# Whole-array sums and masks, and an output projection in two banks, in a recurrent attention kernel

## The chip, the cores and the metric

The kernel runs on one core of a Trainium2 chip. A core has five engines that work side by side and wait for each other through semaphores: TensorE (in the profile PE for matmuls and PEld for the weight loads that go ahead of them), VectorE (DVE), ScalarE (ACT), GpSimd (POOL) and SyncE (SP), which only starts transfers here. Matmuls write to PSUM, which has eight banks of 128 partitions x 512 fp32 numbers; DVE and ACT copy results from there to SBUF. The metric is the device time of one execution in microseconds (us). Three executions of the kernel before took 796.89, 798.72 and 798.89 us, so the median is 798.72 us.

## What is computed

The input x has 2048 rows of 512 numbers. The output is g * a + (1 - g) * b, where g is a sigmoid gate for each row, b is a layer norm followed by a two-layer MLP (512 to 1376 to 512), and a is an attention with a memory, which goes through x in 64 segments of 32 rows:

```
mem = mem0                                   # 8 rows of 512
for s in range(64):
    h = concat(mem, x[32*s : 32*s+32])       # 40 rows
    q, k, v = h @ Wq, h @ Wk, h @ Wv         # 32 heads of 128
    p = softmax(where(mask, q k^T / sqrt(128), -1e9))    # 40 x 40 a head
    o = (p v) @ Wo                           # 4096 -> 512
    mem, out[s] = o[:8], o[8:]
```

The memory rows of one segment are an input of the next one, so the 64 steps form a chain. All matrix inputs are bf16.

## The kernel before

There are two stages. The MLP for all 2048 rows runs first (about 110 us) and leaves (1 - g) * b in DRAM. Then comes the loop over the 64 segments, which is nearly all of the rest. T = s // 4 is the tile of 128 rows that a segment lies in, si = s % 4 its place in the tile.

**Column tiles.** A step's rows are few: 32 (the 8 memory rows and 24 of the segment; the other 8 rows of each of four segments, called left, are projected together once per tile). So most matmuls use only 32 of the array's 128 columns, and four of them are placed side by side with `tile_position=(0, 32 * j)`: each loads 128 x 32 weights into its own quarter of the columns and writes its own 32 PSUM partitions. Four such matmuls are called a quad here. The profile shows a column tile as `128*32`, a matmul over the whole array as `128*128`, and a matmul with 32 contracted rows (a row tile) as `32*128`.

**One step of the loop, in the order of TensorE.** The order of every engine's queue is the order of the program (`manual_schedule`), and each engine works its own queue in order.
- Q and K of the step (`qk_unit`, L110): 16 quads of 512 columns into banks U0 to U3. Between the first four quads and the rest stands `mask_mm(1)` (L248): it writes the additive mask of heads 16 to 31 into bank W, as four column tiles of 224 columns, with a quarter of the identity as weights in each.
- `scores(s, 0)` (L256, L260) adds q k^T onto the mask that lies in bank SbF; ACT takes the exponentials.
- V of the step (`v_unit`, L129), eight quads of 512 columns in banks X1 and X2. After five of these eight, `msum(0)` calls `sums` (L267, L270): two quads with the block-diagonal matrix of ones BO as weights, each of 32 columns, which sum the exponentials over the keys of each of the four heads. DVE takes the reciprocal (L668) and scales E in place (L669). After one more quad of V comes `scores(s, 1)` on bank W, then the last two quads of V, then `msum(1)`.
- `run(W1)`: two quads of side work, `fill`, on banks X1 and X2: projections of the left rows of the next tile (L110, L129), or the output projection of the left rows of the previous tile (L141). A step has eight quads of it, given out two at a time.
- The sums of the other queries (`sums(xsum, ...)`): two quads, of 256 and 64 columns, into SbF.
- `av` (L280, L285): p v in row tiles, in two halves. The second half waits for the scaled E of `mnorm(1)`.
- ACT copies the memory part of U0 to U3 to UT (L697) and then the rest to XR (L598). TensorE does two more quads of side work.
- `wo_pass` (L619): the output projection, eight groups of one quad each (`wo_group`, L141), 512 columns, all into bank W. ACT copies W to w (L622).
- `mask_mm(0)` for the next step, into SbF; two quads of side work; in some steps `extra`: four whole-array transposes of x at si = 3 (L156), or the assembly of a finished output tile at si = 0 (L226 and L228).
- Four whole-array matmuls of 8 columns (L709) with w as weights add up the four partial sums and transpose the memory rows. DVE copies them to hT (L710), which the Q of the next step waits for. The last two quads of side work stand between.

The last step, after the loop, has its own code (L718 to L755): on DVE a reciprocal (L723), two products that scale E (L726, L727), and on TensorE one `wo_pass` for the step before it, ahead of `av`, and another one for itself near the end.

Of the kernel before, what the change touches and what calls it, by code (L numbers as in the profile page):

```python
# [27 lines left out]
def kernel(ctx, tc, A_x, A_mem0, A_Wq, A_Wk, A_Wv, A_Wo, A_seg_len, B_x, B_w1, B_b1, B_w2, B_b2, gate_w, out):  # L28
    nc = tc.nc
    P = 128  # L30
    _, S, Dm = A_x.shape
# [29 lines left out]
    Wo_sb = pers.tile([P, H, Dm], BF16)  # L61
    ident = pers.tile([P, P], BF16)
# [12 lines left out]
    Mk = ep.tile([P, 4, EW], BF16)  # L75
    BO = ep.tile([P, P], BF16)
# [16 lines left out]
    U = [lps.tile([P, 512], FP32, name=f"U{i}") for i in range(4)]  # L93
# [3 lines left out]
    W = lps.tile([P, 512], FP32)  # L97

    Sb = [bk[:, 0:4 * EW].rearrange("p (i c) -> p i c", c=EW) for bk in (SbF, W)]
# [34 lines left out]

    HORD = [(j, ih) for j in (0, 2, 1, 3) for ih in range(2)]

    def wo_group(bk, U_, n):
        j, ih = HORD[n]
        for c in range(4):
            i = 4 * ih + c  # L140
            nc.tensor.matmul(bk[32 * c:32 * c + 32, :], lhsT=U_[:, j, i, :], rhs=Wo_sb[:, 4 * i + j, :],  # L141
                             start=(n == 0), stop=(n == NW - 1), tile_position=(0, 32 * c))

    NW = len(HORD)
# [66 lines left out]
    def wo_left(T, bk):  # L211
        for n in range(NW):
            wo_group(bk, UL[T % 2], n)
            if n < NW - 1:
                yield

        def ca():
            wl = cw.tile([P, Dm], BF16, tag="wl", name="wl")
            nc.scalar.copy(out=wl[:], in_=bk[:])
            wls[T] = wl  # L220
        act_q.append(ca)
        yield
# [21 lines left out]
                              in_=QL[T % 2][:].bitcast(FP32).rearrange("p a (l s) b -> p a l s b", s=SPT)[:, :, :, si])  # L244

    def mask_mm(i2):
        for j in range(4):
            nc.tensor.matmul(Sb[i2][32 * j:32 * j + 32], lhsT=ident[:, 32 * j:32 * j + 32], rhs=Mk[:],  # L248
                             start=True, stop=True, skip_group_check=True, tile_position=(0, 32 * j))

    def scores(s, i2):
        T, si = divmod(s, SPT)
# [10 lines left out]
                             start=False, stop=True, skip_group_check=True, tile_position=(0, 32 * j))  # L263

    def sums(out, E, c_main, c_left, n, start):
        for j in range(4):
            nc.tensor.matmul(out[32 * j:32 * j + 32], lhsT=BO[:, 32 * j:32 * j + 32], rhs=E[:, :, c_main:c_main + n],  # L267
                             start=start, stop=False, skip_group_check=True, tile_position=(0, 32 * j))
        for j in range(4):
            nc.tensor.matmul(out[32 * j:32 * j + 32, :, n - 8:n], lhsT=BO[:, 32 * j:32 * j + 32], rhs=E[:, :, c_left:c_left + 8],  # L270
                             start=False, stop=True, skip_group_check=True, tile_position=(0, 32 * j))

    def av(s, V, E):
        T, si = divmod(s, SPT)
# [286 lines left out]
    nc.gpsimd.memset(rmin[:], 1.0)  # L561

    mask_mm(0)
    Rs = {}
    fill = iter(())
# [50 lines left out]
                                in0=XR[:, :, RIDE:32], in1=Rb[:, :, RIDE:32], op=ALU.mult)  # L616

    def wo_pass(U_):
        for n in range(NW):  # L619
            wo_group(W, U_, n)  # L620
        w = cw.tile([P, Dm], BF16, tag="w", bufs=8, name="w")
        nc.scalar.copy(out=w[:], in_=W[:])  # L622
        return w

    W1, W2, W3 = 2, 2, 2
    for s in range(nseg):
# [17 lines left out]
        for n, (t, hf) in enumerate(((0, 0), (1, 0), (0, 1), (1, 1))):  # L644
            bk = U[n]
            for kc in range(KC):
                qk_unit(bk, hc, t, hf, kc)
            if n == 0:
                flush(act_q, 9)
                mask_mm(1)  # L650
                flush(dve_q, 9)
            qk_tr(qk_cast(bk[:]), (QT, KT)[t], hf)
        V = cw.tile([P, NG, Dh], BF16, tag="V", name="V")
        E = cw.tile([P, NG, EW], BF16, tag="E", name="E")
# [8 lines left out]
        def msum(i2):  # L663
            sums(U[i2][:, 320:352].rearrange("p (i q) -> p i q", q=8), E[:, 4 * i2:4 * i2 + 4, :], 8, 0, 8, True)
# [26 lines left out]
        mnorm(1)  # L691
        run(W1)
        sums(xsum, E, 16, 48, 32, True)
        recip_x(s)
        av(s, V, E)
# [3 lines left out]
        run(W2)  # L699
        prep_q(s + 1)  # L700
        w = wo_pass(UT[s % 2])
        if s >= 1:
            ws[s - 1] = w
        mask_mm(0)
        run(W3)
        for _ in extra(T, si):
# [10 lines left out]

    nx = slice(8 * NG, 40 * NG)  # L718
    sums(xsum, E, 16, 48, 32, True)
    for _ in out_sel(T - 1, X2):  # L720
        pass
    nc.gpsimd.memset(UL[T % 2][:, :, :, LEFT * si:seg], 0.0)
    nc.vector.reciprocal(out=R[:, nx], in_=SbF[:, 0:32 * NG])  # L723
    ws[s - 1] = wo_pass(UT[s % 2])
    Rr = R[:, nx].rearrange("p (i q) -> p i q", q=32)
    nc.vector.tensor_tensor(out=E[:, :, 16:48], in0=E[:, :, 16:48], in1=Rr, op=ALU.mult)  # L726
# [16 lines left out]
    nc.vector.tensor_scalar(out=good[:, 0:1], in0=tot[:, 0:1], scalar1=R_MIN, scalar2=None, op0=ALU.is_gt)  # L743
    nc.vector.tensor_scalar(out=good[:, 1:2], in0=tot[:, 1:2], scalar1=RSUM_MAX, scalar2=None, op0=ALU.is_lt)
    wf = wo_pass(UF)
    nc.tensor.matmul(X1[0:1, 0:1], lhsT=good[:, 0:1], rhs=good[:, 1:2], start=True, stop=True)
    bad = okp.tile([1, 1], I32)
    nc.vector.tensor_scalar(out=bad[:], in0=X1[0:1, 0:1], scalar1=-1.0, scalar2=float(P), op0=ALU.mult, op1=ALU.add)
    nc.tensor.matmul(X2[:], lhsT=SelL[:], rhs=wls.pop(T)[:], start=True, stop=False, skip_group_check=True)
    for i in range(SPT):  # L750
        nc.tensor.matmul(X2[32 * i:32 * i + 32, :], lhsT=(SelR if i < si else SelI)[:], rhs=(ws.pop(SPT * T + i) if i < si else wf)[:],
                         start=False, stop=True, skip_group_check=True, tile_position=(0, 32 * i))
# [126 lines left out]
```

## Time and profile before

One execution was profiled. Its own time was 799.05 us, with 797.3 us from its first to its last instruction.

| | us or count |
|---|---|
| median of the three times | 798.72 |
| profiled execution, own time and span | 799.05 and 797.3 |
| PE busy | 771.9 (97%), 18417 matmuls |
| PEld busy | 421.3 (53%), 18446 loads |
| ACT busy | 578.5 (73%) |
| DVE busy | 444.3 (56%) |
| POOL busy | 260.6 (33%) |
| granted TensorE clock, mean | 0.996 |
| one step of the loop, from one `scores(s, 0)` to the next | 10.89 |

The step's length is the distance of two rows of the trace: the first matmul of `scores` starts at 403.93 us in one step and at 414.82 us in the next.

The lines of the profile are read so. A group of instructions gives its source line, engine and operation, then out<-in by the program's names, the shapes, the count, and the mean time of one; for a matmul that time runs to its modelled end, which is long after the next one can start. A row of the timeline gives a start and a duration in us, the engine, the source line and how many instructions are merged in it; for the pace of TensorE the starts are to be compared, not the durations. A bracket tells how long the engine was idle ahead of the row and what it waited for.

### The profile page before, as it was taken

The numbers are of one execution on the slowest core, as the hardware profiler recorded it, in microseconds if no ns is written. First come the engines' busy times: TensorE is split into PE (matmuls) and PEld (weight loads), VectorE is DVE, ScalarE is ACT, GpSimd is POOL, SyncE is SP. The second block draws the span as 40 slices with busy tenths as digits, with TensorE's granted clock in tenths as the row PEclk, the third lists the DMA queues.
The fourth block names the chain that finished last, engine by engine and source line by source line (L and its number), as shares of the span: only waits on it lengthen the run. The fifth ranks groups of instructions, "written<-read, shape, count | busy, mean of one in ns | idle before, by whom it ended". The sixth has DMA issues, their size and how long they took to land.

```text
span 797.3 us, 41370 instructions
## 1 busy us (share of the span) xinstructions
PE 771.9 (97%) x18417; PEld 421.3 (53%) x18446; DVE 444.3 (56%) x1061; ACT 578.5 (73%) x1440; POOL 260.6 (33%) x391
## 2 busy tenths in 40 slices
PE   7999999999999999999999999999999999999996
PEld 5666554555555555555555555555555555555543
DVE  5776355555555554556555555655465556555554
ACT  4666677777777777777777777777777777777763
POOL 3111133333333334233333334333323333333331
PEclk9999999999999999999999999999999999999999
DMA  5779311212111222211121211222221212121111
GB/s 188 266 275 362 124 51 60 73 60 86 60 64 57 76 70 76 69 56 60 60 86 60 86 59 57 65 76 70 72 74 54 63 59 86 60 80 60 60 53 58
DMA packets 38151, 70.42 MB, mean 88 GB/s; under 512 B 3979, under 2 KB 27888, under 8 KB 36432
## 3 DMA queue, kind: packets, MB, share of 16 engines
q1 hardware_dynamic: 36448, 64.97, 24.6%
q8 instruction: 146, 2.39, 1.3%
q0 software_dynamic: 720, 1.97, 0.7%
q10 hardware_dynamic: 800, 0.79, 0.3%
q14 instruction: 37, 0.30, 0.1%
HBM read 59.06 MB, written 4.45 MB: 80 GB/s over the span
## 4 chain that ended last, share of the span: by engine, by line
PE 93%; ACT 3%; DVE 1%; issue 1%; DMA 1%; POOL 0%; SPq 0%; DVEq 0%; POOLq 0%; ACTq 0%
PE U L110 28%; PE X L129 18%; PE W L141 14%; PE X L110 7%; PE U L468 5%; PE U L280 4%; PE X L141 3%; ACT w L622 3%; PE W L462 3%; PE SbF L462 3%; PE W L709 2%; PE W L256 1%; PE U L267 1%; PE SbF L256 1%; PE SbF L267 1%
## 5 line engine op out<-in xcount | busy, mean ns | idle before, releaser
L115 ACT CAST Tb<-U 128x512 bf16<-128x512 f32 x258 | 195.2, 757 | 43.3 <-PE U L110 24.7
L614 POOL TENSOR_TENSOR UT<-XR,Rb 128x768 bf16<-128x768 bf16 x63 | 104.8, 1664 | 239.1 <-DMA Rb<-r_dr 199.4
L110 PEld LDWEIGHTS <-hT 128*32 128x32 bf16 x4096 | 103.7, 97 | 109.9 <-DVE hT L710 19.2
L129 PE MATMUL X<-Wv_sb,hT 128*32 128x512 bf16 x2048 | 136.4, 378 | 0.0
L110 PE MATMUL U<-Wq_sb,hT 128*32 128x512 bf16 x2048 | 132.7, 379 | 1.1 <-DVE hT L710 1.1
L110 PE MATMUL U<-Wk_sb,hT 128*32 128x512 bf16 x2048 | 132.7, 379 | 0.0
L141 PE MATMUL W<-Wo_sb,UT 128*32 128x512 bf16 x2080 | 124.6, 380 | 1.5 <-ACT UT L697 1.2
L608 POOL TENSOR_TENSOR racc<-racc,R 128x320 f32<-128x320 f32 x63 | 54.5, 866 | 181.9 <-DVE R L603 177.4
L603 DVE RECIPROCAL R<-SbF 128x256 f32<-128x256 f32 x63 | 110.3, 1751 | 0.0
L119 DVE STREAM_TRANSPOSE QT<-Tb 128x256 f32<-128x256 f32 x128 | 57.0, 445 | 80.8 <-ACT Tb L115 80.1
L119 DVE STREAM_TRANSPOSE KT<-Tb 128x256 f32<-128x256 f32 x128 | 57.0, 446 | 54.8 <-ACT Tb L115 54.8
L141 PEld LDWEIGHTS <-UT 128*32 128x32 bf16 x2080 | 57.1, 96 | 57.7 <-issue 19.7
L710 DVE CAST hT<-W 128x32 bf16<-128x32 f32 x63 | 12.1, 192 | 133.3 <-PE W L709 114.8
L598 ACT CAST XR<-U 128x256 bf16<-128x256 f32 x252 | 78.6, 438 | 0.0
L622 ACT CAST w<-W 128x512 bf16<-128x512 f32 x65 | 38.1, 585 | 45.3 <-PE W L141 45.3
L697 ACT CAST UT<-U 128x64 bf16<-128x64 f32 x252 | 35.3, 227 | 43.6 <-PE U L285 43.6
L129 PEld LDWEIGHTS <-hT 128*32 128x32 bf16 x2048 | 46.0, 95 | 20.5 <-issue 0.2
L115 ACT CAST Tb<-X 128x512 bf16<-128x512 f32 x62 | 46.3, 747 | 13.5 <-PE X L110 13.4
L668 DVE RECIPROCAL R<-U 128x32 f32<-128x32 f32 x126 | 45.0, 357 | 16.2 <-PE U L270 9.6
L267 PEld LDWEIGHTS <-BO 128*32 128x32 bf16 x760 | 32.2, 94 | 34.7 <-issue 13.4
L468 PE MATMUL U<-w_sb,hTm 128*128 128x512 bf16 (+1 forms) x163 | 49.5, 381 | 0.6
L462 PEld LDWEIGHTS <-w_sb 128*128 128x128 bf16 (+1 forms) x352 | 34.7, 102 | 21.0 <-issue 4.1
(152 smaller groups left out, 1207.7 us busy)
## 6 DMA issues: line engine op xcount, KB each, us to landing
Rb<-r_dr SPq DMA_DIRECT2D x63, 512.0 KB
Wv_sb<-in_A_Wv_dram SPq DMA_DIRECT2D x4, 1024.0 KB
Wq_sb<-in_A_Wq_dram SPq DMA_DIRECT2D x4, 1024.0 KB
Wk_sb<-in_A_Wk_dram SPq DMA_DIRECT2D x4, 1024.0 KB
Wo_sb<-in_A_Wo_dram SPq DMA_DIRECT2D x4, 1024.0 KB
VP<-VL SPq DMA_DIRECT2D x64, 64.0 KB
xt<-in_A_x_dram SPq DMA_DIRECT2D x16, 128.0 KB
xs<-in_A_x_dram SPq DMA_DIRECT2D x16, 128.0 KB
```

The costliest lines, as they stand in the source:

```text
L110: nc.tensor.matmul(bk[32 * j:32 * j + 32, :], lhsT=G[:, kc, :], rhs=W5[t][:, kc, h0:h1, j, :], start=(kc == 0), stop=(kc == KC - 1), tile_ ...
L115: nc.scalar.copy(out=Tb[:].rearrange("p a e b -> p a b e"), in_=bk.rearrange("p (a b e) -> p a b e", a=8, b=2))
L119: nc.vector.transpose(out=dst[:, 8 * hf:8 * hf + 8, 0:32, :].rearrange("p a r b -> p a (r b)").bitcast(FP32), in_=Tb[:].rearrange("p a e b ...
L129: nc.tensor.matmul(bk[32 * j:32 * j + 32, :], lhsT=G[:, kc, :], rhs=Wv5[:, kc, 4 * vb:4 * vb + 4, j, :], start=(kc == 0), stop=(kc == KC - ...
L141: nc.tensor.matmul(bk[32 * c:32 * c + 32, :], lhsT=U_[:, j, i, :], rhs=Wo_sb[:, 4 * i + j, :], start=(n == 0), stop=(n == NW - 1), tile_po ...
L462: nc.tensor.matmul(hp[:rows, 0:TB * P], lhsT=w1_sb[:, kc, fc * P:fc * P + rows], rhs=yTs[blk][:, kc, :], start=(kc == 0), stop=(kc == KC - 1))
L468: nc.tensor.matmul(bp(blk, tt)[:], lhsT=hTm[blk % 2][:rows, fc, tt * P:(tt + 1) * P], rhs=w2_sb[:rows, fc, :], start=(fc == 0), stop=(fc = ...
L598: nc.scalar.copy(out=XR[:, j], in_=U[j][:, 0:NG * 40].rearrange("p (i q) -> p i q", q=40)[:, :, 8:40])
L603: nc.vector.reciprocal(out=R[:, 8 * NG:], in_=SbF[:, 0:32 * NG])
L608: nc.gpsimd.tensor_tensor(out=racc[:], in0=racc[:], in1=R[:], op=ALU.add)
L614: nc.gpsimd.tensor_tensor(out=UT[(s + 1) % 2][:].rearrange("p j i q -> p (j i) q")[:, :, M:32], in0=XR[:, :, 0:RIDE], in1=Rb[:, :, 0:RIDE] ...
L622: nc.scalar.copy(out=w[:], in_=W[:])
```

## The change

Three functions change.
- `mask_mm` writes the mask with one matmul over the whole array (the 128 x 128 identity as weights) in place of four column tiles. The columns are 224 as before.
- `sums` uses the whole matrix BO as weights: two whole-array matmuls in place of two quads. BO is block-diagonal, so the result is the same.
- `wo_pass` makes the output projection in two passes over the eight groups. The first computes columns 0 to 383 in bank W, the second columns 384 to 511 in bank U0. ACT copies the 384 columns to w once the first pass is done, DVE the 128 columns after the second. The number of matmuls and weight loads of the projection doubles; the columns that they stream stay the same in sum.

```diff
-    def wo_group(bk, U_, n):
+    def wo_group(bk, U_, n, d=slice(0, 512)):
         j, ih = HORD[n]
         for c in range(4):
             i = 4 * ih + c
-            nc.tensor.matmul(bk[32 * c:32 * c + 32, :], lhsT=U_[:, j, i, :], rhs=Wo_sb[:, 4 * i + j, :],
+            nc.tensor.matmul(bk[32 * c:32 * c + 32, 0:d.stop - d.start], lhsT=U_[:, j, i, :], rhs=Wo_sb[:, 4 * i + j, d],
                              start=(n == 0), stop=(n == NW - 1), tile_position=(0, 32 * c))
...
     def mask_mm(i2):
-        for j in range(4):
-            nc.tensor.matmul(Sb[i2][32 * j:32 * j + 32], lhsT=ident[:, 32 * j:32 * j + 32], rhs=Mk[:],
-                             start=True, stop=True, skip_group_check=True, tile_position=(0, 32 * j))
+        nc.tensor.matmul(Sb[i2], lhsT=ident[:], rhs=Mk[:], start=True, stop=True, skip_group_check=True)
...
     def sums(out, E, c_main, c_left, n, start):
-        for j in range(4):
-            nc.tensor.matmul(out[32 * j:32 * j + 32], lhsT=BO[:, 32 * j:32 * j + 32], rhs=E[:, :, c_main:c_main + n],
-                             start=start, stop=False, skip_group_check=True, tile_position=(0, 32 * j))
-        for j in range(4):
-            nc.tensor.matmul(out[32 * j:32 * j + 32, :, n - 8:n], lhsT=BO[:, 32 * j:32 * j + 32], rhs=E[:, :, c_left:c_left + 8],
-                             start=False, stop=True, skip_group_check=True, tile_position=(0, 32 * j))
+        nc.tensor.matmul(out, lhsT=BO[:], rhs=E[:, :, c_main:c_main + n], start=start, stop=False, skip_group_check=True)
+        nc.tensor.matmul(out[:, :, n - 8:n], lhsT=BO[:], rhs=E[:, :, c_left:c_left + 8], start=False, stop=True, skip_group_check=True)
...
     def wo_pass(U_):
-        for n in range(NW):
-            wo_group(W, U_, n)
+
         w = cw.tile([P, Dm], BF16, tag="w", bufs=8, name="w")
-        nc.scalar.copy(out=w[:], in_=W[:])
+        for bk, d, copy in ((W, slice(0, 384), nc.scalar.copy), (U[0], slice(384, Dm), nc.vector.tensor_copy)):
+            for n in range(NW):
+                wo_group(bk, U_, n, d)
+            copy(out=w[:, d], in_=bk[:, 0:d.stop - d.start])
         return w
```

## The prediction

> **What bounds the kernel now.** I read the profile's page first, for the engine that sets the end, then the timeline of TensorE in three stretches of one step, for the pace of its stream and the places where it breaks, and then the waits.
>
> The page gives the engine: TensorE is busy for 97% of the span at a granted clock of 0.996, and carries 93% of the chain that ended last:
>
> ```profile
> PE 93%; ACT 3%; DVE 1%; issue 1%; DMA 1%; POOL 0%; SPq 0%; DVEq 0%; POOLq 0%; ACTq 0%
> ```
>
> The timeline of TensorE shows how little the quads (four column tiles side by side) that the change replaces cost:
>
> ```profile
> 415.81 0.39 PE L129 MATMUL X<-Wv_sb,hT 128*32 128x512 bf16 x4
> 416.03 0.19 PE L267 MATMUL U<-E,BO 128*32 128x32 bf16 x4
> 416.06 0.19 PE L270 MATMUL U<-E,BO 128*32 128x32 bf16 x4
> 416.08 0.39 PE L129 MATMUL X<-Wv_sb,hT 128*32 128x512 bf16 x4
> ...
> 416.48 0.60 PE L129 MATMUL X<-Wv_sb,hT 128*32 128x512 bf16 x8
> 417.00 0.20 PE L267 MATMUL U<-E,BO 128*32 128x32 bf16 x4
> ...
> 417.48 0.29 PE L267 MATMUL SbF<-E,BO 128*32 128x256 bf16 x4
> 417.58 0.21 PE L270 MATMUL SbF<-E,BO 128*32 128x64 bf16 x4
> 417.73 0.27 PE L280 MATMUL U<-E,V 32*128 32x40 bf16 x16
> 417.85 0.19 PE L285 MATMUL U<-E,VP 32*128 32x64 bf16 x4
> 418.02 0.28 PE L280 MATMUL U<-E,V 32*128 32x40 bf16 x16
> ...
> 420.45 0.28 PE L248 MATMUL SbF<-Mk,ident 128*32 128x224 bf16 x4
> 420.55 0.62 PE L110 MATMUL X<-Wk_sb,GL 128*32 128x512 bf16 x8
> 421.33 0.26 PE L709 MATMUL W<-SelM,w 128*128 128x8 bf16 x4 [0.16 <-ACT w L622]
> ```
>
> The starts matter, the durations run into the next rows. A quad of 512 columns takes 0.216 us (415.81 to 416.03), the two quads of `msum(0)` 0.05 together, the 256-column sums 0.10, the mask 0.10 (420.45 to 420.55). Column tile follows column tile without a break. Where the kind of tile changes there is one: the 64-column sums need about 0.03, so the row tiles of `av` could start at 417.61, but start at 417.73.
>
> A step with transposes shows the break to and from whole-array matmuls:
>
> ```profile
> 398.98 0.62 PE L129 MATMUL X<-Wv_sb,GL 128*32 128x512 bf16 x8
> 399.53 0.40 PE L156 MATMUL U<-ident,xs 128*128 128x128 bf16 x4
> 399.76 0.25 PE L709 MATMUL W<-SelM,w 128*128 128x8 bf16 x4
> 399.94 0.40 PE L129 MATMUL X<-Wv_sb,GL 128*32 128x512 bf16 x4
> ...
> 399.52 0.23 PEld L156 LDWEIGHTS <-xs 128*128 128x128 bf16 x4 [0.42 <-issue]
> ```
>
> Two quads from 398.98 end streaming at 399.41, but the transposes start at 399.53, and their weights load only at 399.52: 0.12 us lost going into the whole array. Coming out, the last matmul of L709 starts at 399.85 (0.25 less its own 0.17 behind 399.76) and the next column tile at 399.94: 0.09. The bracket says "issue": nothing that the profile shows was waited for. From whole array (transposes) to whole array (L709) there is no such gap.
>
> The waits have the one place where w holds TensorE up:
>
> ```profile
> PE W L709 <- ACT w L622: 6.7, 35, 0.6
> ```
>
> It counts 35 times, since in the other 28 of 63 steps transposes or the output assembly stand between. Its true size in a usual step comes from the rows above: the two side quads from 420.55 stream until 420.98, the change to whole array takes 0.12, and L709 starts at 421.33, so 0.23 is waited.
>
> **The prices.** Into the whole array: 0.12. Out of it: 0.09 behind the stream, and 0.01 since the first quad after a change takes 0.23. An insertion of whole-array work in column tiles costs 0.22 in changes of tile alone. In a sentence of its own: the Trainium skill says under "TensorEngine Tiling (Array Packing)", section Key Properties, that a change of the tiling mode, not merely of the tile, drains TensorE, and the gaps at 399.41 and 399.85 agree; it gives no size, but "TensorE: Matmul & The Clock Gate", section Single matmul latency, has a fixed part of 398 cycles, 166 ns, for a warm matmul alone, and by an estimate from that page, with as much for each change of tile, the sum below would be some 35 us larger.
>
> **Masks.** Removed: two quads of 0.10 per step. Added: two matmuls of 224 columns, which stream as long (0.10, since four column tiles ran together), and 0.22 each for the changes. The one in Q and K (`mask_mm(1)`) costs 0.22 on the path: no wait of TensorE stands behind it. The one after `wo_pass` (`mask_mm(0)`) costs 0.22 too, but 0.23 of waiting for w stands behind it in 33 of 63 steps.
>
> **msum.** Before 0.05 a call. After: 0.12 in, 0.04 to the second matmul (the first two of L709 start about that far apart, the later ones 0.025), 0.015 to stream it, 0.09 and 0.01 out: 0.27, so +0.22 a call. The first call is followed by a wait of 0.03: the V quad at 416.08 ends at 416.30, `scores(s, 1)` starts at 416.33 when KT is there. It goes: +0.19. The second call already waits 0.09 for ACT's exponentials (two V quads from 416.48 end at 416.91, the sums start at 417.00); the change of tile runs during that wait: +0.13.
>
> **The 320 other sums.** Before, 417.48 to 417.73 with the change to row tiles, 0.25. After: 0.12 in, 0.12 for the first, 0.03 for the second, then whole array to row tiles, which this trace does not show. Bounds: nothing, and 0.12 as from column to row; I take 0.09, the way out of the whole array to column tiles (nearest: same first tile). Sum 0.36, +0.10 (0.01 to 0.14). Less than nothing is excluded, since no change of tile in the trace is free. Behind it, the second half of `av` waits today: the first half is issued until 417.88, it starts at 418.02, when the scaled E of `mnorm(1)` is there. That E becomes ready only 0.03 later than before, as `msum(1)` ends 0.03 later, while TensorE arrives at about 418.13. The wait of 0.14 goes.
>
> **Output projection.** Eight quads of 512 are 1.73. Eight of 384 are 8 x 0.162 = 1.30; eight of 128 are not in the trace as column tiles, bounds 0.03 (64 columns) and 0.10 (224) each; four whole-array transposes of 128 start 0.06 apart, so I take 0.056 and 0.45 in all. Together +0.02. The 32 more weight loads are hidden: in the scores, quads of 40 columns with four loads each start 0.025 apart. ACT's copy of 384 columns, between 0.375 (256, L731) and 0.585 (512, L622), about 0.48, runs during the second pass. DVE's copy of 128 columns lies between 0.192 (32, L710) and 0.419 (256, L731); I take 0.29. DVE starts it 0.23 behind the end of the stream (as ACT does today: 420.45 to 420.69) and L709 sees it 0.05 later: w is whole 0.57 after the projection, today 0.87. With the mask as it was, TensorE would reach L709 0.65 after the projection and the wait of 0.23 would go. With the dearer mask it gets there 0.86 after it, 2.61 after its start; today it is 2.60. So in these 33 steps mask and projection together cost +0.01, in the 28 others 0.22 + 0.02 = 0.24.
>
> What is behind the moved copies: in the loop DVE has only hT, which needs L709 anyway, and the copies of `extra`; ACT's copies of X come later. Bank U0 is long read when the second pass writes it (XR from U0 is the first of four copies, which start at 418.79; the pass starts at 420.03). No transfer, POOL or SP instruction is moved. In the last step DVE's copy stands ahead of the two products L726 and L727: today L726 starts at 785.59, during the projection; then it must wait for the second pass, which ends at 786.17, for 0.23 and for the copy of 0.29, and starts at 786.69. +1.1 once, on the chain. The last projection gains 0.3, the last step's mask costs 0.22: +1.0.
>
> **Sum.** In 33 steps 0.22 + 0.19 + 0.13 + 0.10 - 0.14 + 0.01 = 0.51, 16.8 us. In 28 steps 0.22 + 0.19 + 0.13 + 0.10 - 0.14 + 0.24 = 0.74, 20.7 us. Two steps without side work change tile less and gain 0.3 on w: 0.1 each. The end 1.0. In all 38.7. The profiled execution took 799.05, 0.33 over the median of 798.72; 798.72 + 38.7 is 837.4, and I say 837.5.
>
> **The rivals.**
> 1. *Changes of tile are cheap here.* BO and the identity never change, so their loads wait for no one; if they go in ahead of need, the change costs nothing, and only the gain on w stays: 33 x 0.21 less, 0.5 for the other steps and 0.8 at the end: 793 us, faster. It decides below about 0.04 us for a change (nine changes a step against 0.26 us of waits removed, and 0.21 in 33 steps). For it: L709's and `extra`'s loads follow semaphores. Against it: those had long been given in the transposes' row, and the way out costs 0.09 for weights that have lain ready throughout. 3%. In a sentence of its own: the Trainium skill, "TensorEngine Tiling (Array Packing)", section Instruction Overhead, gives each matmul about 60 cycles, and counted for each of the four tiles the merging would save some 75 ns a quad of sums; the quads at 416.03 and 416.06 do not pay it four times.
> 2. *Half price*, if loads go ahead on the way in or the way out: 0.11 per insertion. The four insertions and the sums then cost 0.48, of which 0.26 goes on waits; in 33 steps w's wait takes the rest, in 28 some 0.24 is left: 7 us and 1 at the end, 807. 5%.
> 3. *The waits come back*: what `scores(s, 1)`, the sums, `av` and L709 wait for also moves later, so nothing of 0.26 us (63 steps) and 0.23 (33 steps) is saved: +24, 861. For it, E of `av` is in time by just 0.08. Against it, all these come from ACT and DVE, which are 73% and 56% busy and get more time. 8%; parts of it are likelier than the whole.
> 4. *A dearer drain*: each of the nine changes waits for the modelled end of the matmul ahead (0.39 long for a stream of 0.216, so 0.17 in place of about 0.11): +34, 871. Against it, the gaps at 399.41 and 399.85 are shorter than that. 2%.
>
> The forecast has 82%. Its unknown prices make +/- 3 us (full to row), 1 (quads of 128), and a misjudged wait of 0.1 us in all steps 6. With parts of rivals 2 and 3: 826 to 850. A change below 0.3% can't be told from none in this kernel. Slower 0.96, same 0.01, faster 0.03.
>
> **What would show it.** Loads of BO and ident as 128x128, starting 0.12 behind the stream of the quad ahead; 0.10 to 0.12 of silence after each; steps of 11.4 and 11.6 us in place of 10.89; L709 waiting for w no more, and no gap in `av`. PE may still read 96% busy, as modelled ends cover such gaps. The forecast is wrong if the loads of BO begin during the quads ahead, or the gaps in `av` and before L709 are still there.

## The result

The changed kernel takes 834.07 us (median; 833.45 to 834.62), the kernel before, in the same comparison, 798.81 us: 1.0439 times as long, with a 95% interval of 1.0424 to 1.0455. The forecast was 837.5 us with a range of 826 to 850, slower. The profiled execution of the changed kernel took 834.62 us, with a span of 832.8 us.

The chain that ended last, on the page of the changed kernel, is now TensorE nearly alone: ACT's 3%, which was the copy of W, is gone.

```profile
PE 97%; DVE 1%; DMA 1%; ACT 0%; issue 0%; POOL 0%; DVEq 0%; POOLq 0%; ACTq 0%
```

The timeline of TensorE in the changed kernel, one step with si = 1 (the columns are start, duration, engine, line, what it is, and how many):

```profile
432.63 0.18 PE L265 MATMUL U<-E,BO 128*128 128x32 bf16 x1
432.73 0.40 PE L129 MATMUL X<-Wv_sb,hT 128*32 128x512 bf16 x4
...
433.09 0.60 PE L129 MATMUL X<-Wv_sb,hT 128*32 128x512 bf16 x8
433.63 0.19 PE L264 MATMUL U<-E,BO 128*128 128x32 bf16 x1
433.67 0.18 PE L265 MATMUL U<-E,BO 128*128 128x32 bf16 x1
433.77 0.62 PE L110 MATMUL X<-Wq_sb,GL 128*32 128x512 bf16 x8
434.32 0.28 PE L264 MATMUL SbF<-E,BO 128*128 128x256 bf16 x1
434.44 0.19 PE L265 MATMUL SbF<-E,BO 128*128 128x64 bf16 x1
434.56 0.27 PE L274 MATMUL U<-E,V 32*128 32x40 bf16 x16
434.68 0.19 PE L279 MATMUL U<-E,VP 32*128 32x64 bf16 x4
434.71 0.29 PE L274 MATMUL U<-E,V 32*128 32x40 bf16 x16
...
435.45 1.48 PE L141 MATMUL W<-Wo_sb,UT 128*32 128x384 bf16 x32
436.74 0.63 PE L141 MATMUL U<-Wo_sb,UT 128*32 128x128 bf16 x32
437.31 0.27 PE L247 MATMUL SbF<-Mk,ident 128*128 128x224 bf16 x1
437.51 0.61 PE L110 MATMUL X<-Wk_sb,GL 128*32 128x512 bf16 x8
438.06 0.26 PE L705 MATMUL W<-SelM,w 128*128 128x8 bf16 x4
```

The two quads of V from 433.09 end streaming 0.43 later, at 433.52; the first sum starts at 433.63, 0.11 after that. The second starts at 433.67 and needs some 0.015, and the next column tiles start at 433.77, 0.09 later. The mask matmul takes from 437.31 to 437.51, 0.20 for a stream of 0.10, after another 0.12 of silence behind the projection (its second pass starts at 436.74 and streams for 8 x 0.056). From the 64-column sums to the row tiles of `av` it is 0.12 with 0.03 of stream, so 0.09.

What waited on the load side of TensorE shows the same thing as a total. The columns are who waited for what, the time in all, how often, and the longest:

```profile
PEld L264 <- issue: 79.3, 187, 0.4
PEld L247 <- issue: 27.2, 64, 0.4
```

The loads of BO and of the identity (L264 and L247) sit idle for 0.42 us each, for nothing that the profile shows, until the quad ahead has left. In the kernel before, the first load of BO started at 415.82, during the quad that starts at 415.81.

The waits that the longer step has swallowed are visible as well: the second half of `av` follows the first at once (434.68 to 434.71; before, 417.85 to 418.02), and the four select matmuls (L705 here, L709 in the kernel before) no longer wait for w: they start 2.61 us after the projection (435.45 to 438.06), as the prediction had it. The copies took what was expected of them:

```profile
L618 ACT CAST w<-W 128x384 bf16<-128x384 f32 x65 | 31.1, 479 | 16.8 <-PE W L141 16.8
L618 DVE CAST w<-U 128x128 bf16<-128x128 f32 x65 | 19.0, 292 | 69.7 <-ACT w L618 68.7 <-PE U L141 0.9
```

### The profile page after: what moved, and what is told of

It is laid out like the page before. It is cut to its first block, busy times and chain, and to the rows that moved or that the text cites. A ratio compares the mean times of both kernels' runs of the same rounds, so it can differ in the third digit from the quotient of the medians.

```text
span 832.8 us, 42640 instructions
## 1 busy us (share of the span) xinstructions
PE 817.9 (98%) x19002; PEld 427.6 (51%) x19002; DVE 464.5 (56%) x1126; ACT 570.4 (68%) x1440; POOL 260.1 (31%) x391
## 4 chain that ended last, share of the span: by engine, by line
PE 97%; DVE 1%; DMA 1%; ACT 0%; issue 0%; POOL 0%; DVEq 0%; POOLq 0%; ACTq 0%
PE U L110 28%; PE X L129 18%; PE W L141 11%; PE X L110 8%; PE U L462 5%; PE X L141 4%; PE U L141 3%; PE U L274 3%; PE W L456 2%; PE SbF L456 2%; PE U L264 2%; PE W L247 2%; PE SbF L264 2%; PE SbF L247 1%; PE W L705 1%; PE SbF L254 1%
## 5 line engine op out<-in xcount | busy, mean ns | idle before, releaser
L110 PEld LDWEIGHTS <-hT 128*32 128x32 bf16 x4096 | 98.4, 96 | 110.0 <-DVE hT L706 19.1
L129 PE MATMUL X<-Wv_sb,hT 128*32 128x512 bf16 x2048 | 141.9, 380 | 0.0
L141 PEld LDWEIGHTS <-UT 128*32 128x32 bf16 x4160 | 93.7, 97 | 44.0 <-issue 21.1
L141 PE MATMUL W<-Wo_sb,UT 128*32 128x384 bf16 x2080 | 96.5, 327 | 1.2 <-ACT UT L693 1.2
L693 ACT CAST UT<-U 128x64 bf16<-128x64 f32 x252 | 35.3, 227 | 47.9 <-PE U L279 47.9
L264 PEld LDWEIGHTS <-BO 128*128 128x128 bf16 x190 | 18.1, 96 | 79.3 <-issue 79.3
L618 DVE CAST w<-U 128x128 bf16<-128x128 f32 x65 | 19.0, 292 | 69.7 <-ACT w L618 68.7
L129 PEld LDWEIGHTS <-hT 128*32 128x32 bf16 x2048 | 45.5, 95 | 22.3
L462 PE MATMUL U<-w_sb,hTm 128*128 128x512 bf16 (+1 forms) x176 | 52.7, 383 | 0.0
L254 PEld LDWEIGHTS <-KT 128*32 128x32 bf16 x2048 | 33.3, 95 | 19.7 <-DVE KT L119 6.1
```

The lines of the kernel that those rows point to most:

```text
L110: nc.tensor.matmul(bk[32 * j:32 * j + 32, :], lhsT=G[:, kc, :], rhs=W5[t][:, kc, h0:h1, j, :], start=(kc == 0), stop=(kc == KC - 1), tile_ ...
L129: nc.tensor.matmul(bk[32 * j:32 * j + 32, :], lhsT=G[:, kc, :], rhs=Wv5[:, kc, 4 * vb:4 * vb + 4, j, :], start=(kc == 0), stop=(kc == KC - ...
L141: nc.tensor.matmul(bk[32 * c:32 * c + 32, 0:d.stop - d.start], lhsT=U_[:, j, i, :], rhs=Wo_sb[:, 4 * i + j, d], start=(n == 0), stop=(n == ...
L264: nc.tensor.matmul(out, lhsT=BO[:], rhs=E[:, :, c_main:c_main + n], start=start, stop=False, skip_group_check=True)
L462: nc.tensor.matmul(bp(blk, tt)[:], lhsT=hTm[blk % 2][:rows, fc, tt * P:(tt + 1) * P], rhs=w2_sb[:rows, fc, :], start=(fc == 0), stop=(fc = ...
```

## The experiments

The theory is that of the forecast: each change between column tiles, whole array and row tiles costs TensorE about 0.1 us, and some of that passes during waits that are there anyway. Its rivals: that whole-array matmuls are dear in themselves, that the waits move along, that the loss lies elsewhere. Times are compared with the kernel before in the same comparison, whose median was 798.88, 799.35 and 800.0 us in the three of them. The two kernels that are derived from the changed one are set against its 834.07 us, which belongs to the comparison with 798.81 (theirs is the one with 799.35); such differences are uncertain by that half microsecond. Where the four-tile form is kept, it is that of the kernel before.

**One mask at a time.** Both kernels are the kernel before with one of the two masks changed; the two masks are the same matmul, only their places differ.

```diff
     def mask_mm(i2):
+        if i2 == 1:      # the second kernel: i2 == 0
+            nc.tensor.matmul(Sb[i2], lhsT=ident[:], rhs=Mk[:], start=True, stop=True, skip_group_check=True)
+            return
         for j in range(4):
```

> Only the mask inside Q and K is a whole-array matmul; all else as before. Theory (a change of tile costs 0.12 us in and 0.10 us out, on the path): 64 x 0.22 = 14 us more, some 812.8 us, steps of 10.91 us in place of 10.69 where nothing else is added. Rival (changes of tile are cheap, the loss of the changed kernel lies elsewhere): 798.8 us.

> Only the mask behind the output projection is a whole-array matmul. Theory (the same 0.22 us, but in 33 of 63 steps it passes during the wait for w): 28 x 0.22 = 6.2 us more, 805 us; the wait of L709's successor for w disappears, the steps with si = 1 and 2 keep their 10.69 us. Rival (the wait for w moves along with it): 63 x 0.22 = 14 us more, 812.7 us.

Measured: 812.91 us for the mask inside Q and K, +14.0 us (ratio 1.0179, 1.0155 to 1.0203), and 804.69 us for the one behind the projection, +5.8 us (1.0068, 1.0044 to 1.0092). The steps with si = 1 and 2 take 10.91 us in the first and 10.69 in the second, against 10.69 before. One operation, two prices: in the second place a wait stands behind it. The timeline of the second kernel, si = 1:

```profile
421.77 1.91 PE L141 MATMUL W<-Wo_sb,UT 128*32 128x512 bf16 x32
423.61 0.27 PE L248 MATMUL SbF<-Mk,ident 128*128 128x224 bf16 x1
423.81 0.62 PE L110 MATMUL X<-Wk_sb,GL 128*32 128x512 bf16 x8
424.37 0.26 PE L712 MATMUL W<-SelM,w 128*128 128x8 bf16 x4
```

From the projection to the select matmuls it is 2.60 us, as before (418.73 to 421.33), though the side work between them starts 0.22 later. That the waits move along (rival 3 of the prediction) is excluded for this one.

**Only the sums.** `sums` as in the change, all else as before.

> Only the sums are whole-array matmuls. Theory (0.22 + 0.22 + 0.10 us of changes of tile a step, of which 0.03 + 0.09 + 0.14 us pass during waits that are there anyway): 63 x 0.28 = 17.6 us more, up to 3 us less where stretched DVE products are hidden as well: 813.5 to 816.5 us, and no gap between the halves of av. Rival (the waits come back behind the longer sums): 63 x 0.54 = 34 us more, 833 us.

Measured: 813.78 us, +14.9 us (1.0184, 1.016 to 1.0207); steps with si = 1 take 10.95 us, 0.26 more than before, where 0.28 was forecast. So nothing of the 0.26 us of waits behind the sums came back. The total is at the lower end of what was expected.

**Twice the mask.** The changed kernel, with each mask matmul issued twice.

```diff
     def mask_mm(i2):
-        nc.tensor.matmul(Sb[i2], lhsT=ident[:], rhs=Mk[:], start=True, stop=True, skip_group_check=True)
+        for _ in range(2):
+            nc.tensor.matmul(Sb[i2], lhsT=ident[:], rhs=Mk[:], start=True, stop=True, skip_group_check=True)
```

> The changed kernel with each whole-array mask matmul issued twice, the second one overwriting the first. Theory (the cost is in the change of tile, not in a whole-array matmul): a second one beside it costs its stream alone, 127 x 0.096 = 12.2 us more than the changed kernel, 846.3 us. Rival (each whole-array matmul is dear, whatever stands beside it): 127 x 0.31 = 39 us more, 873 us.

Measured: 846.97 us, 12.9 us more than the changed kernel's 834.07. A whole-array matmul beside another one costs little more than its stream, for which 12.2 was worked out; 39 us, if each were dear, is excluded. Timeline of TensorE:

```profile
443.45 0.37 PE L248 MATMUL SbF<-Mk,ident 128*128 128x224 bf16 x2
443.75 0.62 PE L110 MATMUL X<-Wk_sb,GL 128*32 128x512 bf16 x8
```

Two of them take 0.30 to the next column tiles, where one took 0.20.

**The mask beside the select matmuls.** The changed kernel, with the mask for the next step behind the four whole-array select matmuls.

```diff
         w = wo_pass(UT[s % 2])
...
-        mask_mm(0)
         run(W3)
...
             nc.tensor.matmul(W[:, M * k:M * k + M], lhsT=w[:, k * P:(k + 1) * P], rhs=SelM[:], start=(k == 0), stop=(k == KC - 1), skip_group_check=True)
+        mask_mm(0)
         nc.vector.tensor_copy(out=hn[:, :, 0:M], in_=W[:, 0:KC * M].rearrange("p (k m) -> p k m", k=KC))
```

> The changed kernel with the mask for the next step moved behind the four select matmuls (L709 in the kernel before), which use the whole array as well; the number of matmuls is the same. Theory (the cost is in the change of tile): two changes less in each of 61 steps, 13.4 us less than the changed kernel, 820.7 us. Rival (each whole-array matmul is dear): as the changed kernel, 834 us.

Measured: 823.11 us, 11.0 us less than the changed kernel, with the same instructions in another order. Of the 13.4 us expected, 2.4 are missing (the four executions took 821.52 to 825.01). The steps tell it better: those with si = 0 and 3 gain 0.20 us, those with si = 1 and 2 0.17 to 0.18, instead of 0.22. The timeline, si = 1:

```profile
430.20 0.62 PE L110 MATMUL X<-Wk_sb,GL 128*32 128x512 bf16 x8
430.75 0.28 PE L704 MATMUL W<-SelM,w 128*128 128x8 bf16 x4
430.89 0.26 PE L247 MATMUL SbF<-Mk,ident 128*128 128x224 bf16 x1
431.08 0.61 PE L110 MATMUL X<-Wk_sb,GL 128*32 128x512 bf16 x8
```

The select matmuls now come 2.29 us after the start of the projection (428.46). One by one they start at 430.75, 430.79, 430.82 and 430.85: the fourth, which needs DVE's part of w (its copy ends at 430.79), comes 0.035 behind the third, where 0.025 is usual, and the mask 0.04 behind the fourth, where it is 0.025 in the steps with si = 0 and 3. That makes the 0.02 to 0.03 by which the two kinds of step differ; that DVE's copy is the cause is likely, not shown. The other 0.02, missing in all steps, is about the 0.025 from one whole-array matmul to the next, which the expected 0.22 did not count.

**Two tiles of 64 columns.** The kernel before, with the mask in Q and K as two column tiles of 64 columns.

```diff
     def mask_mm(i2):
+        if i2 == 1:
+            for j in range(2):
+                nc.tensor.matmul(Sb[i2][64 * j:64 * j + 64], lhsT=ident[:, 64 * j:64 * j + 64], rhs=Mk[:],
+                                 start=True, stop=True, skip_group_check=True, tile_position=(0, 64 * j))
+            return
```

> The mask inside Q and K as two column tiles of 64 columns in place of four of 32; all else as before. Theory (what costs is the change of the tiling, whichever it is): as with one whole-array matmul, 14 us more, 812.8 us. Rival (only the whole array breaks the stream, column tiles of any width follow each other): 798.8 us.

Measured: 813.01 us, +14.1 us (1.0178, 1.0152 to 1.0204), the same as with one whole-array matmul. What TensorE pays for is the change of the tiling, not the whole array. Timeline of TensorE:

```profile
428.69 1.04 PE L110 MATMUL U<-Wq_sb,hT 128*32 128x512 bf16 x16
429.66 0.29 PE L249 MATMUL W<-Mk,ident 128*64 128x224 bf16 x2
429.88 1.05 PE L110 MATMUL U<-Wk_sb,hT 128*32 128x512 bf16 x16
```

The four quads from 428.69 end at 429.55; the tiles of 64 columns start 0.11 later, and hand over 0.22 after their start.

**Only the projection in two banks.** `wo_group` and `wo_pass` as in the change, masks and sums as before; and a second kernel in which the first projection of the last step stays whole.

> Only the output projection is changed (two banks, copies on ACT and DVE); masks and sums in column tiles as before. Theory: the wait of 0.23 us for w goes in 33 steps, 0.02 us more for the stream in all, 0.6 us gained in two steps without side work, and 0.8 us lost at the end where DVE's copy stands ahead of the two products: 793.3 us. Rival (TensorE meets another wait in place of the one for w): 798.8 to 800 us.

> As the split alone, but the first projection of the last step is left whole, copied by ACT, so that no DVE copy stands ahead of the two products that scale E. Theory: 1.1 us less than the split alone, 792.2 us, and L726's counterpart starts during the projection again. Rival (the end is bound by something else): no difference.

Measured: 794.54 us, ratio 0.9932 (0.9919 to 0.9945) to the kernel before: this part of the change alone makes the kernel faster, 5.5 us, as worked out. The timeline, si = 1:

```profile
416.03 1.48 PE L141 MATMUL W<-Wo_sb,UT 128*32 128x384 bf16 x32
417.33 0.63 PE L141 MATMUL U<-Wo_sb,UT 128*32 128x128 bf16 x32
417.77 0.28 PE L248 MATMUL SbF<-Mk,ident 128*32 128x224 bf16 x4
417.87 0.62 PE L110 MATMUL X<-Wk_sb,GL 128*32 128x512 bf16 x8
418.42 0.26 PE L711 MATMUL W<-SelM,w 128*128 128x8 bf16 x4
```

The select matmuls start 2.39 us after the projection, not 2.60, without a wait, and the steps with si = 1 take 10.49 us, not 10.69.

The second kernel, at 794.45 us (0.9934, 0.9919 to 0.9949), doesn't differ, where 1.1 us less was expected; a gain of a few tenths could not be told from none, as the executions of either kernel lie 3 us apart or more. DVE in the last step, of the split alone and then with the first projection whole:

```profile
781.35 0.29 DVE L624 CAST w<-U 128x128 bf16<-128x128 f32 x1 [0.92 <-PE U L141]
781.56 0.41 DVE L728 TENSOR_TENSOR E<-E,R 128x256 bf16<-128x256 bf16 x1
781.89 0.22 DVE L729 TENSOR_TENSOR E<-E,R 128x64 bf16<-128x64 bf16 x1
```

```profile
781.19 0.43 DVE L728 TENSOR_TENSOR E<-E,R 128x256 bf16<-128x256 bf16 x1
781.53 0.75 DVE L729 TENSOR_TENSOR E<-E,R 128x64 bf16<-128x64 bf16 x1
```

The DVE copy does stand ahead of the products, as forecast. But the last product, which starts later for that, takes 0.22 in place of 0.75 us. Counted from the reciprocal (778.68 and 779.33), it ends 3.43 us after it in the first and 2.95 in the second: 0.48 apart, not 1.1. In the second, POOL's addition to `racc` (a running sum of the reciprocals) runs from 781.23 to 782.20, and the stretched product ends 0.08 after it; in the first, that addition is over at 781.31.

**POOL's product out of DVE's way.** In the kernel before, 19 of the 126 products with which DVE scales E (L669) take over 0.3 us, up to 1.10, where 0.23 is usual. Each of the 19 overlaps one of POOL's products. DVE, then POOL, in one step:

```profile
361.57 0.36 DVE L668 RECIPROCAL R<-U 128x32 f32<-128x32 f32 x1
362.03 1.10 DVE L669 TENSOR_TENSOR E<-E,R 128x64 bf16<-128x64 bf16 x1
363.05 0.35 DVE L668 RECIPROCAL R<-U 128x32 f32<-128x32 f32 x1
```

```profile
361.39 1.66 POOL L614 TENSOR_TENSOR UT<-XR,Rb 128x768 bf16<-128x768 bf16 x1 [3.87 <-ACT E L661]
```

The DVE product lasts until just after POOL's, which ends at 363.05. The kernel before was changed so that POOL's second product, UL (the scaled values of the left rows), runs behind its addition to `racc`, when DVE scales nothing:

```diff
-        nc.gpsimd.tensor_tensor(out=UL[T % 2]..., in0=XR[:, :, RIDE:32], in1=Rb[:, :, RIDE:32], op=ALU.mult)
+        later.append(lambda: nc.gpsimd.tensor_tensor(out=UL[T % 2]..., in0=XR[:, :, RIDE:32], in1=Rb[:, :, RIDE:32], op=ALU.mult))
...
+        nc.gpsimd.tensor_tensor(out=racc[:], in0=racc[:], in1=R[:], op=ALU.add)
+        flush(later)
         Rb = cw.tile([P, 4, NG, 32], FP32, tag="Rb", bufs=1, name="Rb")
         nc.sync.dma_start(r_dr[s % 2][:], R[0:P:32, 8 * NG:])
         nc.sync.dma_start(Rb[:]..., r_dr[s % 2][:]...)
-        nc.gpsimd.tensor_tensor(out=racc[:], in0=racc[:], in1=R[:], op=ALU.add)
```

> The kernel before, with POOL's second product (UL, L615) moved behind its addition to racc, so that it no longer runs while DVE scales E (L669). Theory: L669's stretched executions (19 of 126 over 0.3 us) fall to a few, and the delayed halves of av with them: 2 to 3.5 us less, 795.3 to 796.8 us. Rival (POOL has nothing to do with the stretch): as many stretched ones, 798.8 us.

> Split projection with the whole one in the last step, and POOL's UL product moved; masks and sums in column tiles. If all three gains add: 6 + 1 + 2.5 us less, 789.5 us. If the stretched products were already hidden by the missing wait for w: 792 us.

Measured: the stretched products fall from 19 to 4, and those 4 all overlap POOL's first product, UT. The count alone would prove little, since it is 8 in the run with the mask inside Q and K and 22 with the split, where POOL's products stay in place. But in all twelve profiles every stretched product overlaps one of POOL's and ends 0.08 to 0.09 us after it, and where an overlapping product is not stretched, POOL's had at most 0.22 us left when it began. So POOL's product is what holds them up. The time is the same, though: 799.58 against 800.0 us, ratio 0.9994 (0.9982 to 1.0005). The excess of the stretched products fell only from 5.9 to 3.6 us, as three of the four that are left are longer than any in the kernel before, 1.26 to 1.35 us, and make their steps (24, 30 and 41) 0.7 to 0.8 us longer than usual. With the split and the whole last projection, the kernel takes 794.36 us (0.9934, 0.9922 to 0.9947), no better than the split alone, where 789.5 or 792 was expected. The 2 to 3.5 us were not there; the split alone, 794.54 us, is as fast as any kernel tried.

## Why the prediction was right, point by point

**The price of a change of tile** held: 0.12 us in and 0.09 out were read from two rows with transposes and select matmuls in the kernel before, and every new change of tile costs that, the unseen one from whole array to row tiles (0.09 taken) included. Here the rule that changing the tiling mode drains TensorE (the Trainium skill, "TensorEngine Tiling (Array Packing)", section Key Properties) agrees with the runs, the one with tiles of 64 columns above all, which costs 14.1 us. The 166 ns that the Trainium skill gives for a warm matmul alone ("TensorE: Matmul & The Clock Gate", section Single matmul latency) would have been too large for it, against the 0.12 and 0.09 measured. Why a change takes just this long, no run here shows.

**The step** held: 0.51 us more was forecast for the steps where w was waited for and 0.74 for those with transposes or output assembly. The medians are 0.49 (10.69 to 11.18, si = 1) and 0.50 (si = 2), 0.73 (10.89 to 11.62, si = 0) and 0.72 (10.69 to 11.41, si = 3). The forecast lengths of 11.4 and 11.6 us held only in part: they were added to 10.89, which is the length of a step with si = 0, while the others take 10.69. So most of the 33 steps that were to take 11.4 take 11.18, and the 11.41 of the steps with si = 3 meets that number by accident. The parts alone give the same picture: 14.0 us for one mask, 5.8 for the other, 14.9 for the sums, and -5.5 for the projection. They add up to 29.2 and don't have to make 35.3, since the wait for w is counted as a cover in the second mask's run and as a gain in the split's.

**The waits that hide a part** held: the one for w was shown by one mask costing 14.0 and the other 5.8 us; those behind the sums by steps that grow by 0.26 and not by 0.54 us.

**Rivals 1, 2 and 4** fall with the gaps in the changed kernel; rival 3, that the waits come back, falls with the runs of one mask and of the sums.

**The sum** was 3.4 us too high (38.7 against 35.3). Between the two profiled executions it is 35.6: 1.2 up to the first `scores`, for which the prediction has no term (two masks stand there, and this stretch takes 101.1 to 103.5 us in the profiles), 33.7 in the 63 steps of the loop, where 37.7 was forecast, and 0.7 behind the last `scores`, where 1.0 was. So the loop was 4.0 too high, and the 1.2 that was left out hid part of it.

The term that was mis-sized is that of the loop, and there hardly the usual step (0.49 for 0.51, 0.72 for 0.74: some 0.7 us in all) but the unusual ones of the kernel before. I took all 63 for regular. In the profile of before, 13 steps (counted from 0) are 0.09 to 0.60 us longer than usual, 3.3 us in all; in the changed kernel one is, step 22, by 0.47. Steps 12 and 24 (si = 0) last 11.46 and 11.49 us where 10.89 is usual; in the changed kernel they last 11.62, like the others. In these two `av` waits for a product that POOL has stretched: in step 24, whose rows are shown above, it starts at 363.18 instead of right after the sums.

```profile
363.18 0.54 PE L280 MATMUL U<-E,V 32*128 32x40 bf16 x16 [0.20 <-DVE E L669]
```

Three more, 19, 57 and 58, have it too; the five make 1.6 us. In step 4 (0.35) `av` waits for a product that starts late, with no POOL instruction beside it. In the largest of the other seven (1.4 us in all) it is something else: in step 32 (0.32) the last of 16 row tiles of `av` starts at 450.52, 0.33 after the one ahead of it, and the profile shows nothing that it waited for; in step 26 (0.37) the four column tiles of a quad come apart, one starting some 0.2 us behind the other three, from 386.07 up to the select matmuls. Why, stays open. Besides, step 60 was counted with 0.74, but it has no side work; it grew by 0.38.

The changed kernel has 7 stretched products in place of 19, and has more time before `av` needs them. These parts make up the 4.0 us, but each stands on one execution of each kernel, and that avoiding the collisions would gain time is not shown: taking those with UL away in the kernel before did not make it measurably faster.

**The end** was mis-sized too, by less: the DVE copy costs 0.48 and not 1.1 us in the run with the split, because the delayed product no longer meets POOL's addition.

## What to carry to other kernels

Here four column tiles side by side stream in the time of one whole-array matmul (0.10 us either way for 224 columns), so merging them saves no TensorE time; what it costs is the change of tiling, about 0.12 us in and 0.09 out, each time whole-array work is set into a stream of tiles. Group work by tiling, or keep it all in one, and look in the trace for an existing change of tiling to read its price. Before costing an added delay, look for the wait behind it: the same mask cost 14 us in one place and 6 in another; and try the parts of a change alone, for here one part alone gained 5.5 us, while the others alone cost 14.0, 5.8 and 14.9. Finally, look at the spread of the steps, and not only at one of them, before multiplying by their number.

## What was not expected of the hardware

A DVE product with both inputs in SBUF, 0.23 us long, lasts up to 1.10 us in the kernel before when POOL has a product under way: it ends 0.08 to 0.09 us after POOL's does. All 19 stretched ones in the kernel before overlap one, and moving one of POOL's two products away left 4, all with the other product. The Trainium skill states this under "SBUF — State Buffer", section Who interferes with whom: a DVE instruction with two SBUF inputs contends with a GpSimd instruction that reads SBUF; these rows agree. DVE's reciprocals from PSUM (L668), 67 of which overlap POOL's products, stay at 0.34 to 0.36 us.

And a change between column tiles of 32 and of 64 columns costs as much as one to the whole array: 14.1 against 14.0 us for 64 of them.
